# The backward half of a fused S4 and SwiGLU kernel on one Trainium2 core: which engine and which queue does which piece of it

## The chip, the cores and the metric

The kernel runs on one core of one Trainium2 chip. A core has a matrix engine (TensorE, PE in the profile; its weight loads are PEld), VectorE (DVE), ScalarE (ACT), GpSimd (POOL) and a queue engine SyncE (SP). Each runs its own list of instructions in order, and they wait for each other through semaphores. SP, ACT and POOL can issue DMAs, which 16 DMA engines carry out. The metric is the device time of one execution in microseconds (us).

## The reference

Forward and backward of one block on x = A_u of 2048 rows (L) by 576 columns (D):

```python
xn = layernorm(x)
s  = causal_conv(xn, K) + xn * Dskip      # K[d, l] = Re sum_n C exp(dt A l) dt B
h  = silu(xn @ w1) * (xn @ w3)            # 2048 x 4608
g  = silu(h @ w2)
out = x + s * g
```

The state has N = 128 complex entries for each column, and the convolution is causal over all 2048 rows. The outputs are `out` and the gradients of all inputs for a given grad_out: x (out_1), A, B and C, real and imaginary (out_2 to out_7), log dt (out_8), Dskip (out_9), w1, w3 and w2 (out_10 to out_12). Inputs and outputs are bf16, sums are float32.

## The kernel before, in words

The forward comes first: the prologue with layernorm, tables and spectra; the FFN's hidden layer (L719 to L722) beside the generation of the convolution kernel; and the forward tail with the convolution in four quarters of 144 columns, the w2 product (L784) and the transposes of the gradient of the FFN's output into `goT` (L820). The forward leaves in DRAM: the gate and up products (`GI_dram`), h (`H_dram`), spectra of the input and the kernel (`UH_dram`, `KH_dram`), `GS_dram` (the gradient of s), and for the parameters `Q_dram` and `PZ_dram`.

`backward` (L1067) has three strands.

- **The FFN groups.** 4608 hidden columns in 18 groups of FG = 256. `phase6_load` (L1125) brings w2 rows by POOL's queue (`w2r`, L1139) and transposes them on SP (`w2T`, L1123), loads gate and up (`gg_n`, `h_n`) by POOL's queue, and works out silu and its derivative on ACT (L1149, L1151), the gate's factor and h on DVE (L1153, L1154). `phase6_group` (L1157) forms ph = goT x w2T on PE (L1172), empties it on ACT (L1175, `gh`), multiplies on DVE (L1178), stores the two gradients `GU_dram` and `GG_dram`, and makes the weight gradients: w2 (L1200, emptied at L1204) and w1, w3 (L1218, L1227; emptied on ACT at L1221, stored by POOL at L1222).
- **The convolution and the parameters**, woven between the groups. `conv_bwd_quarter` (L866) does a quarter of the columns: it loads spectra (`a3`, variants by DVE at L590 to L592), transforms the gradient (L564, ACT L568), multiplies spectra on DVE (`cmul_acc`, L601 to L610), and transforms back on PE (L582), twice. The first result is the kernel's gradient: 16 tiles of 144 columns a quarter, each written by four strided ACT activations (L926, L927) into `gk_st`, which is stored. The second gives the gradient of xn, added by DVE to `gx` (L947) and stored in `GXN_dram`. `param_quarter` (L950) takes chunks of 16 columns, 36 in all: `qT` is transposed from `Q_dram` on SP, `pz` is loaded by ACT's queue, PE multiplies (L970), DVE multiplies by pz into a tile of 1024 (L977) and reduces it (L979) into `S_all`. After the last chunk `phase5_final` (L984) loads the six rate matrices (L81) and works out for five blocks of columns the gradients of A, B, C and log dt (L996 to L1054).
- **The input stage**, `phase6_inputs` (L1234), after the groups: 16 tiles of 128 rows. The two gradients are transposed from DRAM (`ggc`, `guc`), w1 and w3 are transposed too (12 of 36 chunks early in a pool of their own, `wA`; 24 at the stage's start, `wTB_w`), 144 matmuls sum into `px` (L1262), DVE adds `gxs` (L1265), and `ln_bwd_tile` (L1269 to L1291) finishes the row tile.

What runs first is set by a scheduler at build time: `self.at(us)` sets a priority for what is issued after it, and the order on each engine follows priorities and dependences. `backward(560, 36, 90, 15, 18, ...)` gives these for the groups (36 apart), the convolution's quarters (90), the parameter chunks (15) and the input tiles (18). Tile pools with a number of buffers set when a buffer is free again. `self.dma` alternates SP and ACT.

Of the kernel before, what the change touches and what calls it, by code (L numbers as in the profile page):

```python
# [16 lines left out]
P = 128  # L17
# [43 lines left out]
class K:  # L61
# [246 lines left out]
    def compute_W(self, pool, c, dsz):  # L308
        nc, cfg = self.nc, self.cfg
        N = cfg.N  # L310
        v = slice(0, dsz)
        Wr = pool.tile([P, N], FP32, name="Wr_c")
        Wi = pool.tile([P, N], FP32, name="Wi_c")
        t2 = pool.tile([P, N], FP32, name="Wt2")
        dtc = self.dt_col[v, c:c + 1]
        nc.vector.tensor_tensor(out=Wr[v], in0=self.C_re[v, c, :], in1=self.B_re[v, c, :], op=ALU.mult)
        nc.vector.tensor_tensor(out=t2[v], in0=self.C_im[v, c, :], in1=self.B_im[v, c, :], op=ALU.mult)
        nc.vector.tensor_tensor(out=Wr[v], in0=Wr[v], in1=t2[v], op=ALU.subtract)
        nc.vector.tensor_scalar(out=Wr[v], in0=Wr[v], scalar1=dtc, scalar2=None, op0=ALU.mult)
        nc.vector.tensor_tensor(out=Wi[v], in0=self.C_re[v, c, :], in1=self.B_im[v, c, :], op=ALU.mult)  # L320
        nc.vector.tensor_tensor(out=t2[v], in0=self.C_im[v, c, :], in1=self.B_re[v, c, :], op=ALU.mult)
        nc.vector.tensor_tensor(out=Wi[v], in0=Wi[v], in1=t2[v], op=ALU.add)
        nc.vector.tensor_scalar(out=Wi[v], in0=Wi[v], scalar1=dtc, scalar2=None, op0=ALU.mult)
        return Wr, Wi

# [262 lines left out]
    def spectrum_variants(self, A2, Az):  # L588
        nc = self.nc
        nc.vector.tensor_copy(out=A2[:, :, 1], in_=A2[:, :, 0])  # L590
        nc.vector.tensor_copy(out=A2[0:1, :, 1, 0, :], in_=Az[0:1, :, 0, :])
        nc.vector.memset(Az[0:1, :, 0, :], 0.0)  # L592

# [245 lines left out]
    def ssm_bwd_conv(self, T0, TQ, ps):  # L839
# [3 lines left out]
        with self.tc.tile_pool(name="b_k", bufs=1, side="right") as kp, self.tc.tile_pool(name="b_z", bufs=2, side="right") as zp:  # L843
            self.at(T0)
            self.lcol = kp.tile([P, LT], FP32, name="lcol")
            nc.vector.tensor_scalar(out=self.lcol[:], in0=self.irow[:, 0:LT], scalar1=float(P),
                                    scalar2=self.pcol[:, 0:1], op0=ALU.mult, op1=ALU.add)
            nc.vector.tensor_scalar(out=self.lcol[:], in0=self.lcol[:], scalar1=1.0 / 512, scalar2=None, op0=ALU.mult)
            self.ones_col = kp.tile([P, 1], BF16, name="ones_col")
            nc.vector.memset(self.ones_col[:], 1.0)  # L850
            for g in range(4):
                self.conv_bwd_quarter(g, kp, zp, ps, T0 + g * TQ, TQ)

    def ssm_bwd_params(self, T0, TC, S_all, ps):
        cfg = self.cfg
        D, LT = cfg.D, cfg.LT
        with self.tc.tile_pool(name="g_k", bufs=1, side="right") as gkp, self.tc.tile_pool(name="g_q", bufs=2, side="right") as qp:
# [5 lines left out]
            for g in range(4):  # L863
                self.param_quarter(g, gz, S_all, qp, ps, T0 + TC * g * D // 64, TC)

    def conv_bwd_quarter(self, g, kp, zp, ps, T0, TQ):  # L866
# [10 lines left out]
        for b in range(NB):  # L877
            a3 = kp.tile([P, 3, KT, W], BF16, name=f"a3_{b}")
            nc.sync.dma_start(out=a3[:, 1], in_=self.UH_dram[g, b, :, 0])
            nc.sync.dma_start(out=a3[:, 0], in_=self.UH_dram[g, b, :, 1])  # L880
            A2[b], Az[b] = a3[:, None, 1:3], a3[:, None, 0]
            self.spectrum_variants(A2[b], Az[b])
# [6 lines left out]
        for b in range(NB):  # L889
            prod = zp.tile([P, KT, W], BF16, name="gsxn")  # L890
            for tt in range(KT):
                t = b * KT + tt
                nc.vector.tensor_tensor(out=prod[:, tt, :].rearrange("p (h d) -> p h d", h=2),
# [12 lines left out]
        for i in range(NB - 1, -1, -1):  # L906
            self.at(T0 + TQ * (0.2 + 0.1 * (NB - 1 - i)))
# [12 lines left out]
            for oc in range(KT):  # L920
                t = i * KT + oc
                pt = ps.tile([P, 512], FP32, name="et_ps")
                self.idft_tile(pt, ZZ, oc)
                for h in range(2):
                    pv = pt[:, h * W // 2:(h + 1) * W // 2].rearrange("p (c d) -> p c d", d=8)
                    nc.scalar.activation(out=st[:, :, 0, :, h, t], in_=pv, func=ACT.Copy, scale=1.0 / 512)  # L926
                    nc.scalar.activation(out=st[:, :, 1, :, h, t], in_=pv, func=ACT.Copy, scale=self.lcol[:, t:t + 1])  # L927
# [7 lines left out]
        for j in range(NB):  # L935
            self.at(T0 + TQ * (0.6 + 0.1 * j))
# [3 lines left out]
            gx = zp.tile([P, KT, W], FP32, name="gx")  # L940
            nc.vector.tensor_tensor(out=gx[:], in0=gs[:, j * KT:(j + 1) * KT, :],
                                    in1=self.dskip_row[:, None, cs].to_broadcast([P, KT, W]), op=ALU.mult)
            for oc in range(KT):
                t = j * KT + oc
                pt = ps.tile([P, 512], FP32, name="et_ps")
                self.idft_tile(pt, Z, oc)
                nc.vector.tensor_tensor(out=gx[:, oc, :], in0=pt[:, 0:W], in1=gx[:, oc, :], op=ALU.add)  # L947
            nc.scalar.dma_start(out=self.GXN_dram[:, j * KT:(j + 1) * KT, cs], in_=gx[:])

    def param_quarter(self, g, gz, S_all, qp, ps, T0, TC):  # L950
# [3 lines left out]
        for cc in range(NQ):  # L954
# [6 lines left out]
            qT = qp.tile([P, 16, N], BF16, name="qT")  # L961
            self.nat_transpose(qT[:], self.Q_dram[ch])
            pz = qp.tile([P, 3, 16, AV], BF16, name="pz")
            nc.scalar.dma_start(out=pz[:], in_=self.PZ_dram[:, ch])
            for h in range(2):
# [8 lines left out]
                for s in range(2):  # L974
                    pr = qp.tile([P, 2, 8, 2, AV], FP32, name="pr_q")
                    for r in range(2):
                        nc.vector.tensor_tensor(out=pr[:, r], in0=T[r][:], in1=pz[:, s + r, h * 8:h * 8 + 8, :][:, :, None, :]  # L977
                                                .to_broadcast([P, 8, 2, AV]), op=ALU.mult)
                    nc.vector.tensor_reduce(out=S_all[:, 2 * s:2 * s + 2, d0:d0 + 8].rearrange("p k d -> p d k"),  # L979
                                            in_=pr[:].rearrange("p r d k a -> p d k r a"), op=ALU.add, axis=AX.XY)  # L980

    def phase5_final(self, out, big, S_all, ps2):
        nc, cfg = self.nc, self.cfg
        D, DT, N = cfg.D, cfg.DT, cfg.N  # L984
        aps = self.aps
        fp = out.enter_context(self.tc.tile_pool(name="gf", bufs=2, side="right"))
        fo = out.enter_context(self.tc.tile_pool(name="gfo", bufs=3, side="right"))
        pp = out.enter_context(self.tc.tile_pool(name="gfp", bufs=1, side="right"))
        if True:
            self.load_rates(pp)  # L990
            glogdt = big.tile([P, DT], FP32, name="glogdt")
            nc.vector.memset(glogdt[:], 0.0)
            for c, (do, dsz) in enumerate(cfg.dch):
                pt = ps2.tile([P, 4, N], FP32, name="et_ps")
                for kd in range(4):
                    nc.tensor.transpose(pt[0:dsz, kd, :], S_all[:, kd, do:do + dsz], self.ident_f[:])  # L996
                ST = fp.tile([P, 4, N], FP32, name="ST")
                nc.scalar.copy(out=ST[0:dsz], in_=pt[0:dsz])
                v = slice(0, dsz)
                S1r, S2r, S1i, S2i = ST[v, 0, :], ST[v, 1, :], ST[v, 2, :], ST[v, 3, :]  # L1000
                Wr_t, Wi_t = self.compute_W(fp, c, dsz)
                Wr, Wi = Wr_t[v], Wi_t[v]
                dtc = self.dt_col[v, c:c + 1]
                grho = fp.tile([P, N], FP32, name="grho")
                gth = fp.tile([P, N], FP32, name="gth")
                t1 = fp.tile([P, N], FP32, name="ft1")
                nc.vector.tensor_tensor(out=grho[v], in0=Wr, in1=S2r, op=ALU.mult)
                nc.vector.tensor_tensor(out=t1[v], in0=Wi, in1=S2i, op=ALU.mult)
                nc.vector.tensor_tensor(out=grho[v], in0=grho[v], in1=t1[v], op=ALU.subtract)
                nc.vector.tensor_tensor(out=gth[v], in0=Wr, in1=S2i, op=ALU.mult)  # L1010
                nc.vector.tensor_tensor(out=t1[v], in0=Wi, in1=S2r, op=ALU.mult)
                nc.vector.tensor_tensor(out=gth[v], in0=gth[v], in1=t1[v], op=ALU.add)
                nc.vector.tensor_scalar(out=gth[v], in0=gth[v], scalar1=-1.0, scalar2=None, op0=ALU.mult)
                for src, oname in ((grho, "out_2"), (gth, "out_3")):
                    ob = fo.tile([P, N], BF16, name="gout")
                    nc.vector.tensor_scalar(out=ob[v], in0=src[v], scalar1=dtc, scalar2=None, op0=ALU.mult)
                    self.dma(aps[oname][do:do + dsz, :], ob[v])
                acc1 = fp.tile([P, 1], FP32, name="acc1")
                acc2 = fp.tile([P, 1], FP32, name="acc2")
                junk = fp.tile([P, N], FP32, name="junk")  # L1020
                nc.vector.tensor_tensor_reduce(out=junk[v], in0=grho[v], in1=self.A_re[v, c, :], scale=1.0, scalar=0.0,
# [366 lines left out]
```

## Time and profile before

| | us |
|---|---|
| median of 2 runs | 2061.51 (2052.20 to 2070.82) |
| the profiled execution | 2058.91 |
| its span | 2057.1 |
| FFN groups, first to last weight-gradient store | 794 to 1642 |
| convolution backward | about 800 to 1320 |
| parameter chunks | 1319 to 1990 |
| input stage, px matmuls | 1656 to 2017.4 |
| POOL w2r L1139 waiting for w2T transposes | 122.1 |
| ACT gw L1221 waiting for out_dram<-gw | 40.0 |

All times are from one execution. A busy time is the sum of the durations of an engine's instructions; a wait is idle time of an engine put down to what released it. A group of instructions is named by its line, engine, operation and tiles. The mean granted clock of TensorE was 0.947 of full speed.

### The profile page before, as it was taken

How to read it: one execution, taken by the hardware profiler on the slowest of the kernel's cores; microseconds unless marked ns; L12 is line 12 of the kernel's file. 1: busy time of each engine (PE TensorE's matmuls, PEld its weight loads, DVE VectorE, ACT ScalarE, POOL GpSimd, SP SyncE). 2: the span in 40 equal slices, each digit the busy share in tenths (PEclk: the TensorE clock that was granted, in tenths of full speed). 3: DMA queues.
4: the chain of work that ended last, by engine and by line, in shares of the span. 5: the costliest groups of instructions: out<-in, count | busy, mean ns of one | idle time of the engine just before them, and what ended most of it. 6: DMA issues, size and time to landing. Idle time of an engine off the chain costs nothing. (4 is left out here: it accounts for less than half of the span.)

```text
span 2057.1 us, 42197 instructions
## 1 busy us (share of the span) xinstructions
PE 1772.9 (86%) x17174; PEld 1300.8 (63%) x17174; DVE 1428.3 (69%) x2772; ACT 992.8 (48%) x1668; POOL 366.5 (18%) x540
## 2 busy tenths in 40 slices
PE   2889999999699995999898998898899939989992
PEld 1534444444488874778777777786678727767771
DVE  7548888888287723686874868676789635858667
ACT  2778888888445544765646556343355200000000
POOL 4003333333312102111111211222111200000000
PEclk9999999999799997999999999999899969999996
DMA  3678888896957568465563655798898599999970
GB/s 83 204 290 301 306 298 302 290 320 248 283 140 175 136 139 260 125 179 168 165 179 96 195 155 164 196 264 205 183 208 203 163 232 216 198 216 226 208 150 22
DMA packets 595505, 416.06 MB, mean 202 GB/s; under 512 B 404912, under 2 KB 537136, under 8 KB 590704
## 3 DMA queue, kind: packets, MB, share of 16 engines
q1 hardware_dynamic: 539632, 264.00, 53.6%
q0 software_dynamic: 30544, 120.94, 17.2%
q10 hardware_dynamic: 25136, 28.44, 5.5%
q8 instruction: 134, 2.20, 0.4%
q14 instruction: 59, 0.48, 0.1%
HBM read 133.01 MB, written 188.01 MB: 156 GB/s over the span
## 5 line engine op out<-in xcount | busy, mean ns | idle before, releaser
L719 PE MATMUL pgu<-wmB_w,xnT 128*128 128x512 bf16 x1152 | 284.1, 382 | 1.1 <-ACT E_k L392 1.1
L1262 PE MATMUL px<-wTB_w,guc 128*128 128x288 bf16 x1152 | 243.7, 292 | 36.4 <-DMA guc<-GU_dram 24.1
L1262 PE MATMUL px<-wTB_w,ggc 128*128 128x288 bf16 x1152 | 245.3, 292 | 15.0 <-DMA wTB_w<-in_B_w_dram 9.1
L1218 PEld LDWEIGHTS <-xn_bf 128*128 128x128 bf16 x2304 | 226.2, 98 | 48.7 <-issue 20.7
L977 DVE TENSOR_TENSOR pr_q<-et_ps,pz 128x512 f32<-128x512 f32 x288 | 186.6, 680 | 96.2 <-PE et_ps L970 96.0
L1172 PE MATMUL ph<-w2T,goT 128*128 128x256 bf16 x1440 | 192.3, 286 | 8.8 <-ACT gh L1175 6.5
L719 PEld LDWEIGHTS <-xnT 128*128 128x128 bf16 x1152 | 103.5, 98 | 125.2 <-issue 20.9
L1279 ACT ACTIVATE t<-gx 128x576 f32<-128x576 f32 x16 | 10.9, 683 | 346.0 <-DVE gx L1265 311.3
L979 DVE TENSOR_REDUCE S_all<-pr_q 128x16 f32<-128x1024 f32 x144 | 173.9, 1211 | 0.4
L1200 PE MATMUL pgw<-go_o,h_n 128*128 128x288 bf16 x1152 | 160.9, 294 | 8.7 <-DVE h_n L1154 8.7
L1172 PEld LDWEIGHTS <-goT 128*128 128x128 bf16 x1440 | 144.1, 103 | 33.8 <-issue 7.8
L1262 PEld LDWEIGHTS <-guc 128*128 128x128 bf16 x1152 | 114.1, 100 | 68.9 <-DMA guc<-GU_dram 26.1
L1221 ACT CAST gw<-pgw 128x256 bf16<-128x256 f32 x144 | 53.7, 378 | 212.5 <-PE pgw L1218 169.7
L784 PE MATMUL po<-w2g,hc 128*128 128x288 bf16 x1152 | 148.9, 286 | 2.6 <-DMA hc<-H_dram 2.6
L1218 PE MATMUL pgw<-gg_n,xn_bf 128*128 128x256 bf16 x1152 | 132.5, 276 | 14.2 <-ACT gw L1221 14.2
L1262 PEld LDWEIGHTS <-ggc 128*128 128x128 bf16 x1152 | 113.8, 100 | 45.4 <-issue 9.6
L1200 PEld LDWEIGHTS <-h_n 128*128 128x128 bf16 x1152 | 113.9, 100 | 39.0 <-DVE h_n L1154 9.2
L1218 PE MATMUL pgw<-gu_n,xn_bf 128*128 128x256 bf16 x1152 | 132.3, 272 | 3.4 <-ACT gw L1221 2.0
L784 PEld LDWEIGHTS <-hc 128*128 128x128 bf16 x1152 | 111.5, 98 | 30.2 <-DMA hc<-H_dram 3.1
L722 ACT ACTIVATE s_t<-pgu 128x512 bf16<-128x512 f32 x144 | 87.4, 609 | 55.2 <-PE pgu L721 54.7
L1222 POOL DMA_DIRECT2D out_dram<-gw x144 | 77.7, 541 | 187.1 <-ACT gw L1221 184.0
L1175 ACT CAST gh<-ph 128x512 bf16<-128x512 f32 x144 | 83.7, 613 | 50.8 <-PE ph L1172 35.9
(305 smaller groups left out, 3726.1 us busy)
## 6 DMA issues: line engine op xcount, KB each, us to landing
GI_dram<-gu_t POOLq DMA_DIRECT2D x72, 512.0 KB, 5.7
H_dram<-h_t SPq DMA_DIRECT2D x72, 256.0 KB, 5.2
Q_dram<-q_k SPq DMA_DIRECT2D x36, 512.0 KB, 5.3
gg_n<-GI_dram POOLq DMA_DIRECT2D x18, 1024.0 KB, 5.7
h_n<-GI_dram POOLq DMA_DIRECT2D x18, 1024.0 KB, 8.7
GU_dram<-gu_n SPq DMA_DIRECT2D x36, 512.0 KB, 4.2
GG_dram<-gg_n SPq DMA_DIRECT2D x36, 512.0 KB, 7.5
E_dram<-E_k SPq DMA_DIRECT2D x18, 768.0 KB, 3.6
```

The lines of the kernel that those rows point to most:

```text
L719: nc.tensor.matmul(pgu[:, j], lhsT=xnT[:, c, ts], rhs=wm[w][:, c, :], start=(c == 0), stop=False)
L722: nc.scalar.activation(out=s_t[:, :, q, :], in_=pgu[:, 0].rearrange("p (g f) -> p g f", g=ng), func=ACT.Silu)
L784: nc.tensor.matmul(pos[k][:, pi_, 0:pw], lhsT=hcs[k][:, fi, :], rhs=w2[fi][:, po:po + pw], start=(fi == 0), stop=(fi == FT - 1))
L977: nc.vector.tensor_tensor(out=pr[:, r], in0=T[r][:], in1=pz[:, s + r, h * 8:h * 8 + 8, :][:, :, None, :] .to_broadcast([P, 8, 2, AV]), op= ...
L979: nc.vector.tensor_reduce(out=S_all[:, 2 * s:2 * s + 2, d0:d0 + 8].rearrange("p k d -> p d k"), in_=pr[:].rearrange("p r d k a -> p d k r ...
L1172: nc.tensor.matmul(ph[j][:, k, :].rearrange("p (a f) -> p a f", f=P), lhsT=lw, rhs=rh, start=(n == 0), stop=(n == nfull))
L1175: nc.scalar.copy(out=gh[:, j], in_=ph[j][:])
L1200: nc.tensor.matmul(pgw[pi_][:, 0:pw], lhsT=hn[:, tt, fl * P:(fl + 1) * P], rhs=go_o[:, tt, po:po + pw], start=(tt == 0), stop=(tt == LT - 1))
L1218: nc.tensor.matmul(pw_[:, 0:FG], lhsT=self.xn_bf[:, tt, c * P:(c + 1) * P], rhs=nat[:, tt, :], start=(tt == 0), stop=(tt == LT - 1))
L1221: nc.scalar.copy(out=gw[:], in_=pw_[:, 0:FG])
L1222: nc.gpsimd.dma_start(out=aps[oname][c * P:(c + 1) * P, fb:fb + FG], in_=gw[:])
L1262: nc.tensor.matmul(px[pi_][:, 0:pw], lhsT=act[:, fi, :], rhs=wT[part][ai][:, f, po:po + pw], start=(fi == 0 and ai == 0), stop=(fi == FT - ...
```

## The change

In `backward` and what it calls:

- w2: no row loads, no `w2r`; two fixed `w2T` buffers, transposed from DRAM on SP: 512 columns of a row block by one transpose, the other 64 by a second call (it is built as an ordinary copy whose source steps 576 elements).
- h: the DVE product of silu and up (L1154) goes; after the gate's factor is made, `h_n` is loaded again, now from `H_dram`, by POOL's queue.
- Queues: gate and up loads, and all stores of weight gradients, from POOL to ACT; the four full column blocks of a w1 or w3 gradient are collected and stored at once; `pz` from ACT to SP; `GXN_dram` stores from ACT to SP, in two halves.
- Convolution: a third load in place of two DVE copies, with one row fixed by POOL; products `gsxn` and `gx` on POOL; transforms back in pairs of tiles in one PSUM bank; the kernel's gradient written densely by ACT (`gk_sd`) and put into `gk_st` order by POOL; new priorities.
- Parameters: POOL adds the two halves of `pr_q`, DVE reduces 512 elements; three `qT` buffers; `final_block` runs for a block of columns as soon as its chunks are done, with its rates loaded by POOL's queue, in place of `phase5_final` at the end.
- Input stage: 9 chunks of w1 and w3 early, 27 at its start; DVE adds in place into `gxs`, without a permutation.
- `backward(560, 40, 96, 15, 18, ...)`.

The core of the diff (`spectrum_variants` held the three DVE instructions of L590 to L592; in `final_block` the arithmetic is that of `phase5_final` and is left out):

```diff
@@ conv_bwd_quarter
-            nc.sync.dma_start(out=a3[:, 1], in_=self.UH_dram[g, b, :, 0])
-            nc.sync.dma_start(out=a3[:, 0], in_=self.UH_dram[g, b, :, 1])
+            for j, r in ((0, 1), (1, 0), (2, 0)):
+                nc.sync.dma_start(out=a3[:, j], in_=self.UH_dram[g, b, :, r])
-            self.spectrum_variants(A2[b], Az[b])
+            nc.gpsimd.tensor_copy(out=a3[0:1, 2, 0, :], in_=a3[0:1, 0, 0, :])
+            nc.gpsimd.memset(a3[0:1, 0, 0, :], 0.0)
...
-                nc.vector.tensor_tensor(out=prod[:, tt, :].rearrange("p (h d) -> p h d", h=2),
+                nc.gpsimd.tensor_tensor(out=prod[:, tt, :].rearrange("p (h d) -> p h d", h=2),
...
-            for oc in range(KT):
-                t = i * KT + oc
+            sd = sp.tile([P, KT, 2, W], BF16, name="gk_sd")
+            for o2 in range(0, KT, 2):
+                t = i * KT + o2
                 pt = ps.tile([P, 512], FP32, name="et_ps")
-                self.idft_tile(pt, ZZ, oc)
+                for j in range(2):
+                    self.idft_tile(pt[:, j * W:(j + 1) * W], ZZ, o2 + j)
+                nc.scalar.activation(out=sd[:, o2:o2 + 2, 0, :], in_=pt[:, 0:2 * W].rearrange("p (t d) -> p t d", t=2),
+                                     func=ACT.Copy, scale=1.0 / 512)
+                for j in range(2):
+                    nc.scalar.activation(out=sd[:, o2 + j, 1, :], in_=pt[:, j * W:(j + 1) * W], func=ACT.Copy,
+                                         scale=self.lcol[:, t + j:t + j + 1])
+            for k in range(2):
                 for h in range(2):
-                    pv = pt[:, h * W // 2:(h + 1) * W // 2].rearrange("p (c d) -> p c d", d=8)
-                    nc.scalar.activation(out=st[:, :, 0, :, h, t], in_=pv, func=ACT.Copy, scale=1.0 / 512)
-                    nc.scalar.activation(out=st[:, :, 1, :, h, t], in_=pv, func=ACT.Copy, scale=self.lcol[:, t:t + 1])
+                    nc.gpsimd.tensor_copy(out=st[:, :, k, :, h, i * KT:(i + 1) * KT],
+                                          in_=sd[:, :, k, h * W // 2:(h + 1) * W // 2].rearrange(
+                                              "p t (c d) -> p c d t", d=8))
...
-            nc.vector.tensor_tensor(out=gx[:], in0=gs[:, j * KT:(j + 1) * KT, :],
+            nc.gpsimd.tensor_tensor(out=gx[:], in0=gs[:, j * KT:(j + 1) * KT, :],
...
-                nc.vector.tensor_tensor(out=gx[:, oc, :], in0=pt[:, 0:W], in1=gx[:, oc, :], op=ALU.add)
-            nc.scalar.dma_start(out=self.GXN_dram[:, j * KT:(j + 1) * KT, cs], in_=gx[:])
+                nc.vector.tensor_tensor(out=gx[:, o2:o2 + 2, :], in0=pt[:, 0:2 * W].rearrange("p (t d) -> p t d", t=2),
+                                        in1=gx[:, o2:o2 + 2, :], op=ALU.add)
+            for h in range(2):
+                nc.sync.dma_start(out=self.GXN_dram[:, j * KT:(j + 1) * KT, :].rearrange(
+                    "p t (h g d) -> p t h g d", h=2, g=4)[:, :, h, g], in_=gx[:, :, h * W // 2:(h + 1) * W // 2])
@@ param_quarter
-            qT = qp.tile([P, 16, N], BF16, name="qT")
+            qT = tqp.tile([P, 16, N], BF16, name="qT")
-            nc.scalar.dma_start(out=pz[:], in_=self.PZ_dram[:, ch])
+            nc.sync.dma_start(out=pz[:], in_=self.PZ_dram[:, ch])
...
+                    nc.gpsimd.tensor_tensor(out=pr[:, 0], in0=pr[:, 0], in1=pr[:, 1], op=ALU.add)
                     nc.vector.tensor_reduce(out=S_all[:, 2 * s:2 * s + 2, d0:d0 + 8].rearrange("p k d -> p d k"),
-                                            in_=pr[:].rearrange("p r d k a -> p d k r a"), op=ALU.add, axis=AX.XY)
+                                            in_=pr[:, 0], op=ALU.add, axis=AX.X)
+            self.at(T0 + TC * (cc + 2))
+            ready(ch)
@@ final_block
+        for i, n in enumerate(("A_A_re", "A_A_im", "A_B_re", "A_B_im", "A_C_re", "A_C_im")):
+            nc.gpsimd.dma_start(out=X[v, i, :], in_=aps[n][do:do + dsz, :])
@@ backward
-        FA = 12
+        FA = 9
+            self.w2T = [wp.tile([P, self.FG // P, cfg.DT, P], BF16, name=f"w2T{i}") for i in range(2)]
@@ phase6_load
-            nc.gpsimd.dma_start(out=w2r[:, 0:D], in_=aps["B_w2"][fi * P:(fi + 1) * P, :])
-            self.nat_transpose(w2T[:, fl], w2r[:])
+            self.nat_transpose(w2T[:, fl, 0:nfull], aps["B_w2"][fs, 0:nfull * P])
+            self.nat_transpose(w2T[0:rem, fl, nfull], aps["B_w2"][fs, nfull * P:D])
-        nc.gpsimd.dma_start(out=gg[:], in_=self.GI_dram[gi, :, 0])
-        nc.gpsimd.dma_start(out=hn[:], in_=self.GI_dram[gi, :, 1])
+        nc.scalar.dma_start(out=gg[:], in_=self.GI_dram[gi, :, 0])
+        nc.scalar.dma_start(out=hn[:], in_=self.GI_dram[gi, :, 1])
...
-            nc.vector.tensor_tensor(out=hn[:, sl, :], in0=gu[:, sl, :], in1=hn[:, sl, :], op=ALU.mult)
+        nc.gpsimd.dma_start(out=hn[:], in_=self.H_dram[:, :, gi * FG:(gi + 1) * FG].rearrange("t p f -> p t f"))
@@ phase6_grad13
+            gw = gwp.tile([P, nfull, FG], BF16, name="gw13")
...
-                nc.scalar.copy(out=gw[:], in_=pw_[:, 0:FG])
-                nc.gpsimd.dma_start(out=aps[oname][c * P:(c + 1) * P, fb:fb + FG], in_=gw[:])
+                nc.scalar.copy(out=gw[:, c, :], in_=pw_[:, 0:FG])
+            nc.scalar.dma_start(out=aps[oname][0:nfull * P, fb:fb + FG].rearrange("(c p) f -> p c f", p=P), in_=gw[:])
```

## The prediction

> **What bounds the kernel now.** I read the page first (busy shares, slices, costliest groups), then a table of windows by stage, then what TensorE (PE) waited for in each stage, then the chain of work that ended last. The page:
>
> ```profile
> PE 1772.9 (86%) x17174; PEld 1300.8 (63%) x17174; DVE 1428.3 (69%) x2772; ACT 992.8 (48%) x1668; POOL 366.5 (18%) x540
> ```
>
> PE is the bound; VectorE (DVE) at 69% isn't, so its removed work is worth only what PE waits for it. By stage (columns: PE, PE load, DVE, ACT, POOL busy with counts, granted clock, DMA share, GB/s):
>
> ```profile
> 800.00:1320.00 520.00, 462.54 (x4663) 394.89 (x4662) 370.07 (x770) 315.59 (x714) 92.40 (x167) 0.96 0.56 167
> 1320.00:1645.00 325.00, 289.85 (x3004) 243.59 (x3001) 240.81 (x336) 139.97 (x234) 64.61 (x118) 0.96 0.89 206
> 1645.00:1720.00 75.00, 34.26 (x271) 24.68 (x272) 31.57 (x45) 0.78 (x2) 0.00 (x0) 0.70 1.14 229
> 1720.00:2017.00 297.00, 281.57 (x2604) 223.52 (x2602) 205.41 (x399) 13.06 (x32) 0.00 (x0) 0.98 1.07 194
> 2017.00:2057.00 40.00, 0.72 (x6) 0.33 (x4) 27.16 (x145) 1.50 (x5) 0.00 (x0) 0.56 0.09 20
> ```
>
> The rows are the FFN groups with the conv backward; the groups with the parameters; the start of the input stage; its steady part; the tail. PE idles 57.5, 35.2, 40.7, 15.4 and 39.3 us in them: 188 us is all that any edit here can win. What PE waited for between 700 and 1645:
>
> ```profile
> PE et_ps L582 <- ACT gk_st L927: 20.7, 22, 3.2
> PE pgw L1218 <- ACT gw L1221: 16.2, 8, 5.0
> PE et_ps L970 <- DMA qT<-Q_dram: 14.7, 4, 8.9
> PE ptr L820 <- DVE goT L824: 12.1, 4, 9.4
> PE et_ps L582 <- DVE gx L947: 9.8, 4, 3.6
> PE pgw L1200 <- DVE h_n L1154: 8.7, 1, 8.7
> PE ph L1172 <- ACT gh L1175: 6.5, 5, 2.6
> ```
>
> Columns: us in total, times, longest. The first, fifth and sixth are aimed at directly. The tail, from the chain:
>
> ```profile
> 1991.64 0.41 SPq L81
> 1992.10 3.76 DMA A_im_bf<-in_A_A_im_dram
> 1995.87 2.52 DMA C_re_bf<-in_A_C_re_dram
> ...
> 2037.20 0.20 DVE gr L1043
> ...
> 2042.15 0.59 DVE t L1286
> 2042.76 0.77 DVE t L1289
> 2043.55 0.82 DVE o L1291
> ```
>
> After the last parameter reduction the six rate matrices are loaded, then DVE does all five blocks of phase5_final from 1998 to about 2040, in front of the last layernorm tile. The last px matmul ends at 2017.4, so 39.7 us are tail.
>
> **What the Trainium skill says.** "DMA: Bandwidth & Descriptors", Rules for kernel authors: an access pattern whose last dim isn't contiguous becomes one descriptor per element. Same page, Issuing engines are not separate DMA queues: moving a DMA to another engine's queue saves only issue time; the 16 engines stay shared. Same page, Bandwidth (Measured): about 10.5 ns per packet, a price used below. "SBUF — State Buffer", Who interferes with whom: a DVE instruction with two SBUF inputs and a GpSimd (POOL) instruction that reads SBUF block each other. The trace of before agrees with the second in that the input stage's DMA share stays near 1.1 whatever queue issues; it shows none of the others clearly.
>
> **The change, part by part.**
>
> (1) Tail. Each of the five final blocks is issued as soon as its last chunk is reduced, and in PE's program order the parameters now end 4.85 tiles (4.85 x 20.8 us, from 15 px tiles in 311 us) before the end. The last block's loads (3.8+2.5 us) and its fifth of the 42 us of DVE work lie under px matmuls. Left behind the last px: L1265 twice 0.45, L1282 0.75, L1285 0.14, L1286 0.57, L1289 0.75, L1291 0.81 = 3.9, the store about 5.2 (median landing of out_dram<-o), about 1 to close: 10. **39.7 - 10 = -30.** If the parameters end late, the cover is gone and up to 8 us (one block) come back.
>
> (2) Kernel gradients (64 idft tiles). Before: 128 activations at 0.815 and 128 at 0.791 = 162 us of ACT, strided. After: per pair one dense 128x288 (L676 is 0.40) and two 128x144 (L568 is 0.32): 32 x 1.04 = 33 us; POOL does the strided step in 64 copies, off PE's path because only the gK store, then the parameters, want it. Their cost isn't in the trace: between 0.5 us (POOL's smallest copies) and 1.9 us (POOL's 128x640 adds reach 1950 ns), 32 to 122 us of a POOL busy 92 of 520. The 20.7 us of waits go, but PE then meets DVE's product chain: I take **-15**. The halved gx adds (32 at 0.45 for 64 at 0.30): of 9.8 **-6**.
>
> (3) h. 72 DVE products at 0.68 (48 us) become 18 POOL-issued loads of 1 MB, and the single 8.7 us wait of pgw on h_n: **-6**. The load lands in 5.7 to 8.7 us (GI rows) and is wanted half a group (23 us) later. Behind it in POOL's order stand gsxn, gk copies and later the pr adds; it waits for DVE's gg product, a few us.
>
> (4) Weight gradients. 144 + 36 + 36 stores leave POOL (144 x 0.541 = 78 us of issue) for ACT as 36 + 36 + 36, and so do the 36 GI loads. ACT waited 40.0 us for out_dram<-gw with gw's buffers; with three times larger tiles and fewer stores, PE's 16.2 falls by **-10**. New: 144 issues at about 0.55 us (ACTq 619 ns at L81) = 79 us on the engine that empties PSUM, each of which may wait for an earlier transfer. ACT drops 129 in (2), and its busy share in these stages is 61 and 43%: average room is there, moments aren't: **+8**.
>
> (5) Other DVE relief in the conv: gsxn (10.1), gx products (11.8), the copies at L590-592 (8.7) go to POOL or to 16 more UH loads. Nothing directly, as PE rarely waits there; two-input DVE products (L601-610, some 220 us) and POOL's reads of SBUF now block each other; up to half of POOL's new 60 to 150 us could return: **+4**, since DVE is busy only 370 of 520.
>
> (6) Parameters. 144 reductions of 1024 at 1.21 become 512, about 0.65: DVE -80 us; 144 POOL adds of 128x512 f32, near 1.53 (its 128x640 f32 add): 220 us over the 671 us from 1319 to 1990, 6.1 per chunk of 18.6, so POOL isn't the pace. PE waits for pr_q only 0.9 and 3.6: **-3**. The third qT buffer against 14.7: **-5**. Moving pz to SP adds 36 issues to a queue that carries transposes of 3.4 to 5.7 us each: **+3**.
>
> (7) Input stage. wB grows from 24 to 27 chunks of 36: the ten transposes at the start took SP 33.8 us, 12.5% more is **+4**. The contiguous add at L1265: nothing, since DVE waits 114 us for px there.
>
> (8) w2. The row loads and SBUF transposes (1.2 us of SP each) become a DRAM transpose of 512 columns and, for the other 64, a copy whose source steps 576 elements: 128 x 64 = 8192 two-byte elements, 512 per engine if spread over 16, 36 such copies. The w2T buffers are filled a group ahead (47 us), so only traffic counts. Price: 10.5 ns gives 5.4 us each; the mean packet of queue q1 (53.6% of 16 x 2057.1 over 539632 packets) is 33 ns, 17 us each. The one like it before, the load of log_dt (32 two-byte elements per engine), landed in 2.3 us where the quickest 16 KB load took 2.0, so 9 ns; counted against a 1.5 us store it is 25. I take 10.5, and keep 5 to 17 us. Room: the stages of transposes hold a share of 1.14, so the parameter groups have 1.14 x 325 - 0.89 x 325 = 81 us of engine time. In them fall 14 copies, 7 reloads of h (2048 packets of 512 B, 33 ns, over 16: 4.2 us each, 30) less 14 row loads and transposes (about 2 us each, 28). So 14 copies fit up to (81 - 2)/14 = 5.6 us each, and above that each us costs 14/1.14 = 12.3 us. At 5.4 they just fit: **+3**.
>
> Sum: -30 -15 -6 -6 -10 +8 +4 -3 -5 +3 +4 +3 = -53; 2058.9 - 53 = 2006. The conv stage has 57.5 us idle and DVE lighter by about 60 of 370, so some of the small unnamed waits go too: -6. 2000 on the profiled run's scale; the median shown, 2061.5, is 2.6 above it, within the spread of its two runs, and is taken as the same.
>
> **Rivals.** *Small packets become the bound (slower).* At 17 us the parameter groups overshoot by (14 x 17 + 2 - 81)/1.14 = 139 us, the conv groups (22 copies, 593 - 291 us of room) by about 65: 2058.9 + 204 - 53 = 2210. It eats the gain from 5.6 + 56/12.3 = 10.2 us a copy (20 ns an element) and costs 2% from 13.7 us (27 ns). For it: the share is 1.14 already at 1320-1390 and through the input stage. Against: the log_dt load. *Only the tail (same):* PE in the groups stands at 0.89 busy and ACT's new queue returns what gk_st gave: 2058.9 - 30 + 4 = 2033; the six small sources of idle make it possible. *Everything bites:* of 92.7 us of idle in the groups 75 go with the tail: 2059 - 105 = 1954; against it, gh and goT (18.6) aren't touched, and a wait removed on PE uncovers the next producer in the same chain. *The edit on DVE does nothing* is the second case: DVE is never PE's long wait.
>
> **Numbers.** Likeliest case (1965 to 2020) 0.43; everything bites 0.12; only the tail or partly slowed copies (2020 to 2103) 0.22; packets bound 0.23. A measurement of this kernel can tell about 2% from no change, 2020 to 2103. Faster 0.55, same 0.22, slower 0.23. The likeliest's own range is 1965 to 2020; for 8 in 10, 1948 to 2125.
>
> **What would show it.** Right: the tail after the last px near 10 us; no wait on gk_st; L979 near 0.65 us; DVE about 200 us lower; w2T copies landing within 8 us and the share in the parameter groups near 1.1. Wrong: w2T copies landing in 15 us or more, with PE waiting for w2T, qT or guc; PE waiting for ACT while ACT waits for a DMA; pr adds well above 2 us.

## The result and the profile after

The changed kernel takes 2411.95 us (median of 2 runs, 2410.19 to 2413.72) against 2061.51: a ratio of 1.17, 95% interval 1.147 to 1.193. It was forecast at 2000, with 1948 to 2125 as the range; the forecast had the wrong sign. Ratios leave out single runs over 1.5% above the fastest of the same kernel; medians of runs include them. The page after, in the lines that answer to those shown of before:

```profile
PE 1837.2 (76%) x17174; PEld 1330.5 (55%) x17174; DVE 1352.9 (56%) x2538; ACT 939.3 (39%) x1508; POOL 624.3 (26%) x653
...
q1 hardware_dynamic: 849152, 283.42, 70.2%
```

VectorE (DVE) was unloaded less than its share, 69 to 56%, suggests: its busy time fell by 75 us (1428.3 to 1352.9), where the prediction named about 200 as a sign of being right; the rest of the fall is the longer span. It bought nothing: TensorE (PE) fell from 86 to 76%, though its own busy time rose by 64 us while its mean granted clock went from 0.947 to 0.893. Queue q1 carries 309,520 more packets for 19 MB more.

By stage (same columns as before; the groups with the convolution, the groups with the parameters, the start of the input stage, its rest, the tail):

```profile
800.00:1500.00 700.00, 500.13 (x4733) 418.29 (x4733) 353.48 (x574) 272.83 (x568) 187.47 (x192) 0.84 0.99 143
1500.00:1975.00 475.00, 319.84 (x3038) 256.25 (x3038) 228.77 (x388) 134.09 (x228) 123.13 (x106) 0.84 1.07 160
1975.00:2040.00 65.00, 26.88 (x215) 19.07 (x216) 21.96 (x35) 0.00 (x0) 15.19 (x12) 0.66 1.09 218
2040.00:2404.00 364.00, 294.49 (x2594) 229.88 (x2593) 192.70 (x459) 13.66 (x34) 94.77 (x98) 0.92 0.97 160
2404.00:2412.00 8.00, 0.32 (x3) 0.01 (x1) 3.90 (x8) 0.78 (x2) 0.00 (x0) 0.81 0.07 24
```

The convolution's part went from 520 to 700 us, and its DMA share from 0.56 to 0.99 while its GB/s fell from 167 to 143: more busy, moving less. From the first ph to the last weight gradient the groups grew from 847 to 1176 us. The input stage, first px to last, grew from 361 to 417. The tail is 8 us, from 39.7. What PE waited for between 700 and 1975:

```profile
PE ph L1169 <- ACT gh L1172: 74.9, 13, 24.0
PE pgw L1216 <- ACT gw L1218: 70.5, 10, 14.7
PE ph L1169 <- DMA w2T<-in_B_w_dram: 28.2, 2, 20.0
```

The columns are the total in us, the number of waits and the longest. Only the third names w2T. But waits of up to 24 us for ACT, whose copies last 0.6 us, are not ACT's own: something held ACT. SP's queue engine at one such place (start, duration, what):

```profile
1008.50 0.65 SPq L1121 DMA_DIRECT2D w2T<-in_B_w_dram  x1
1009.20 15.89 SPq L1121 DMA_TRANSPOSE w2T<-in_B_w_dram  x1
1025.18 1.47 SPq L874 DMA_DIRECT2D a<-UH_dram  x3
```

The copy of 8192 two-byte elements is issued in 0.65 us, and the transpose behind it can't be issued for 15.9 us, nor anything behind that. The 36 copies and the 36 transposes of w2T land after 15.8 us in the median (2.6 to 22.3); the transposes of the kernel before took 3.2. What a copy does to the rest is plainest where it met little else. This one is issued at 1310.51; the windows of the core, and then all DMA packets from 1312 to 1319:

```profile
1308.00:1312.00 4.00, 4.00 (x36) 3.32 (x34) 4.00 (x8) 2.82 (x3) 3.37 (x1) 1.00 0.85 200
1312.00:1316.00 4.00, 3.01 (x32) 2.52 (x31) 4.00 (x8) 1.77 (x4) 4.00 (x1) 1.00 1.62 3
1316.00:1320.00 4.00, 2.90 (x30) 2.36 (x28) 4.00 (x8) 0.00 (x0) 3.94 (x3) 1.00 1.84 12
...
DMA packets 7904, 0.02 MB, mean 2 GB/s; under 512 B 7904, under 2 KB 7904, under 8 KB 7904
```

For 7 us 7904 packets move 0.02 MB, which is the copy's 8192 two-byte elements but for 288; nothing else moves, though ACT issues a store at 1313.66 and SP stands at the next transpose for 7.42 us from 1311.23. The copy at 1008.50 shared its time with other transfers, and there SP stood longer.

### The profile page after: what moved, and what is told of

Read it like the earlier page. It is cut to its first block, busy times and chain, and to the rows that moved or that the text cites. A ratio compares the mean times of both kernels' runs of the same rounds, so it can differ in the third digit from the quotient of the medians.

```text
span 2411.9 us, 42058 instructions
## 1 busy us (share of the span) xinstructions
PE 1837.2 (76%) x17174; PEld 1330.5 (55%) x17174; DVE 1352.9 (56%) x2538; ACT 939.3 (39%) x1508; POOL 624.3 (26%) x653
## 3 DMA queue, kind: packets, MB, share of 16 engines
q10 hardware_dynamic: 41312, 62.71, 10.5%
## 4 chain that ended last, share of the span: by engine, by line
PE 17%; DMA 15%; DVE 12%; SPq 7%; issue 4%; POOL 3%; ACT 2%; ACTq 0%; POOLq 0%; DVEq 0%
PE px L1258 5%; PE pgw L1216 5%; SPq L1121 5%; DMA w2T<-in_B_w_dram 4%; DMA out_dram<-gout 3%; DMA pz<-PZ_dram 3%; POOL pr_q L989 2%; DVE pr_q L987 2%; PE pgw L1197 2%; PE ph L1169 2%; DVE cm_t L583 1%; DVE S_all L990 1%; DMA a<-KH_dram 1%; PE et_ps L546 1%; DVE cm_t L580 1%
## 5 line engine op out<-in xcount | busy, mean ns | idle before, releaser
L989 POOL TENSOR_TENSOR pr_q<-pr_q 128x512 f32<-128x512 f32 x144 | 190.2, 1323 | 504.1 <-DVE pr_q L987 414.9
L1216 PEld LDWEIGHTS <-xn_bf 128*128 128x128 bf16 x2304 | 238.3, 104 | 147.0 <-issue 106.2
L1169 PE MATMUL ph<-w2T,goT 128*128 128x256 bf16 x1440 | 208.5, 299 | 104.0 <-ACT gh L1172 74.9
L1258 PE MATMUL px<-wTB_w,guc 128*128 128x288 bf16 x1152 | 248.5, 295 | 24.1 <-DMA wTB_w<-in_B_w_dram 12.3
L1197 PE MATMUL pgw<-go_o,h_n 128*128 128x288 bf16 x1152 | 168.6, 299 | 29.7 <-DMA h_n<-H_dram 15.8
L1216 PE MATMUL pgw<-gu_n,xn_bf 128*128 128x256 bf16 x1152 | 148.5, 291 | 54.5 <-DVE gu_n L1175 23.1
L1216 PE MATMUL pgw<-gg_n,xn_bf 128*128 128x256 bf16 x1152 | 144.1, 288 | 47.4 <-ACT gw L1218 47.4
L1274 ACT ACTIVATE t<-gxs 128x576 f32<-128x576 f32 x16 | 11.0, 684 | 387.4 <-DVE gxs L1261 373.6
L990 DVE TENSOR_REDUCE S_all<-pr_q 128x16 f32<-128x512 f32 x144 | 98.8, 686 | 100.7 <-POOL pr_q L989 100.7
L704 POOL DMA_DIRECT2D GI_dram<-gu_t x72 | 68.7, 954 | 216.4 <-DVE gu_t L700 171.4
```

What stands on the lines that cost most here:

```text
L704: nc.gpsimd.dma_start(out=self.GI_dram[fb * ng:(fb + 1) * ng, :, :, i0:i0 + NT, :].rearrange("g p u t f -> p u g (t f)"), in_=gu_t[:].rear ...
L989: nc.gpsimd.tensor_tensor(out=pr[:, 0], in0=pr[:, 0], in1=pr[:, 1], op=ALU.add)
L1169: nc.tensor.matmul(ph[j][:, k, :].rearrange("p (a f) -> p a f", f=P), lhsT=lw, rhs=rh, start=(n == 0), stop=(n == nfull))
L1197: nc.tensor.matmul(pgw[pi_][:, 0:pw], lhsT=hn[:, tt, fl * P:(fl + 1) * P], rhs=go_o[:, tt, po:po + pw], start=(tt == 0), stop=(tt == LT - 1))
L1216: nc.tensor.matmul(pw_[:, 0:FG], lhsT=self.xn_bf[:, tt, c * P:(c + 1) * P], rhs=nat[:, tt, :], start=(tt == 0), stop=(tt == LT - 1))
L1258: nc.tensor.matmul(px[pi_][:, 0:pw], lhsT=act[:, fi, :], rhs=wT[part][ai][:, f, po:po + pw], start=(fi == 0 and ai == 0), stop=(fi == FT - ...
```

## The experiments

Theory 1: the element copies' own time on the DMA engines. Theory 2: ACT, issuing DMAs now, is blocked. Theory 3: POOL's new work stands in the way. Each group of runs was timed beside its own runs of the kernel before (medians 2037 to 2054 us), so between groups I compare ratios.

**Same bytes, whole runs.**

```diff
-            self.nat_transpose(w2T[0:rem, fl, nfull], aps["B_w2"][fs, nfull * P:D])
+            nc.sync.dma_start(out=w2T[0:rem, fl, nfull], in_=aps["B_w2"][(gi * nfl + fl) * P:(gi * nfl + fl) * P + rem, 0:P])
```

> The changed kernel with the 64-column remainder of w2 copied as 64 contiguous runs of 256 bytes instead of 8192 two-byte elements; same bytes, queue, semaphores and count, but the wrong values of w2 land there, so the w2 remainder of ph is not the reference's. Theory 1 (the elements' time on the 16 DMA engines, about 36 x 16 us, sets the loss): falls by over 300 us, to 1990 to 2080, and w2T copies land in under 5 us. Theory 2 (ACT blocked by issuing DMAs): falls only by what ACT waits for w2T, 88 us, to about 2320. Theory 3 (final blocks and pr adds on POOL hold up the input stage): the input stage stays near 430 us long, total not below 2100.

Measured: 2179.73 us, ratio 1.0627 (1.0558 to 1.0696). q1 in this run:

```profile
q1 hardware_dynamic: 556544, 283.42, 56.1%
```

Against the changed kernel that is 292,608 packets (36 x (8192 - 64), one an element) and 0.702 x 2411.9 - 0.561 x 2179.2 = 471 us of all 16 engines less: an estimate of 25.7 ns a packet, 13 us a copy, in the sum of packet times. The w2T copies and transposes now land after 3.4 us in the median. Of the loss, 0.107 of the ratio goes with the elements, some 220 us, where theory 1 had forecast over 300; some 130 us do not, and the input stage is still 415 us long, so theory 3 has a share.

**w2's rows as before**, in the changed kernel.

```diff
-            self.nat_transpose(w2T[:, fl, 0:nfull], aps["B_w2"][fs, 0:nfull * P])
-            self.nat_transpose(w2T[0:rem, fl, nfull], aps["B_w2"][fs, nfull * P:D])
+            nc.gpsimd.dma_start(out=w2r[:, 0:D], in_=aps["B_w2"][fi * P:(fi + 1) * P, :])
+            self.nat_transpose(w2T[:, fl], w2r[:])
```

> The changed kernel with w2's row loads by POOL and transposes from SBUF as before; all else as changed. Theory 1: within 20 us of the contiguous-copy run, 1990 to 2080. Theory 2: about 2320. Theory 3: above 2100, with the loss in the input stage.

Measured: 2192.02, ratio 1.0689 (1.061 to 1.0768): like the contiguous copy, above theory 1's range.

**The w2 edit alone**, on the kernel before (the diff above, reversed).

> The kernel before with only the w2 edit (transposes from DRAM and the element copies on SP, two fixed buffers). Theory 1: slower than before by 200 to 350 us, 2260 to 2410. Theory 2 (needs ACT's new DMAs): loses under 100 us, below 2160.

Measured: 2303.20, ratio 1.1218 (1.1121 to 1.1315): some 250 us lost without any of ACT's new DMAs. PE waits 79.5 us for gh here too, and 29.5 for w2T.

**ACT's DMAs back on POOL**, copies kept.

```diff
-        nc.scalar.dma_start(out=gg[:], in_=self.GI_dram[gi, :, 0])
+        nc.gpsimd.dma_start(out=gg[:], in_=self.GI_dram[gi, :, 0])
...
-            nc.scalar.dma_start(out=aps["out_12"][fi * P:(fi + 1) * P, :], in_=gw2[:])
+            nc.gpsimd.dma_start(out=aps["out_12"][fi * P:(fi + 1) * P, :], in_=gw2[:])
```

> The changed kernel with gate and up loads and all weight-gradient stores back on POOL's queue, element copies kept. Theory 1: gains under 60 us, above 2350. Theory 2: gains 150 us or more, below 2260.

Measured: 2434.66, ratio 1.187 (1.1789 to 1.195): no gain. Theory 2 falls: with POOL issuing, w2T still lands after 16.2 us in the median.

**The remaining 130 us.** In the contiguous-copy run the input stage shows idle stretches of all engines. Its windows (PE, PE load, DVE, ACT, POOL busy; clock; DMA share; GB/s):

```profile
1952.00:1956.00 4.00, 4.00 (x34) 3.06 (x32) 2.31 (x10) 0.64 (x2) 1.02 (x2) 1.00 2.56 105
1956.00:1960.00 4.00, 0.13 (x2) 0.00 (x0) 0.44 (x1) 0.00 (x0) 1.10 (x3) 1.00 1.85 2
1960.00:1964.00 4.00, 0.00 (x0) 0.00 (x0) 0.00 (x0) 0.00 (x0) 0.00 (x0) 0.68 1.45 2
1964.00:1968.00 4.00, 0.00 (x0) 0.00 (x0) 0.00 (x0) 0.00 (x0) 0.00 (x0) 0.50 1.13 35
```

and what POOL had issued just before, with SP's transpose that then hung:

```profile
1947.63 0.54 POOL L1059 DMA_DIRECT2D out_dram<-gl  x1 [0.17 <-issue]
...
1950.73 0.56 POOL L1039 DMA_DIRECT2D out_dram<-gout  x1 [0.39 <-DVE gout L1036]
1950.74 21.22 SPq L1121 DMA_TRANSPOSE guc<-GU_dram  x1
```

The DMA engines count as busy over 100% and move 2 GB/s. Two suspects: POOL's queue (the stores of `gout`), or the store of `gl`, the block's gradient of log dt, 128 two-byte elements written to DRAM by each of the five final blocks. First I took the first:

```diff
-            nc.gpsimd.dma_start(out=aps[oname][do:do + dsz, :], in_=ob)
+            self.dma(aps[oname][do:do + dsz, :], ob)
...
-                tc.tile_pool(name="gfo", bufs=2, side="right") as fo:
+                tc.tile_pool(name="gfo", bufs=3, side="right") as fo:
```

> The changed kernel with w2's rows as before and the final blocks' gradient stores alternating between SP and ACT with three buffers instead of two, not on POOL. Theory 3a (a store issued by POOL among transposes lands after up to 18 us, and DVE waits for its buffer, 71 us in the contiguous-copy run): input stage shorter by 45 to 70 us, total 2125 to 2150. Rival (the stores only fill time in which PE is held by the serial chain of DVE product, POOL add, DVE reduction): under 15 us, above 2175.

Measured: 2282.32, ratio 1.1162 (1.1116 to 1.1209): some 90 us slower than with rows alone, outside both. On top of it, the reduction back on DVE:

```diff
-                    nc.gpsimd.tensor_tensor(out=pr[:, 0], in0=pr[:, 0], in1=pr[:, 1], op=ALU.add)
-                                            in_=pr[:, 0], op=ALU.add, axis=AX.X)
+                                            in_=pr[:].rearrange("p r d k a -> p d k r a"), op=ALU.add, axis=AX.XY)
```

> The one with rows and final stores as before, and the pr_q halves no longer added on POOL (DVE reduces 1024 elements as before). Theory 3b (the POOL add stands in series: two products 1.2, add 1.3, reduction 0.7 make 3.2 us a step against 2.6): another 30 to 60 us less, about 2080 to 2110; PE's wait for pr_q falls from over 40 us to under 10. Rival (DVE's load matters, and POOL takes 80 us off it): slower by 10 to 40.

then `nc.gpsimd` to `nc.vector` at gsxn, gx and the row fixes:

> The one with the reduction on DVE, and also gsxn, the gx products and the two row fixes of the spectra back on DVE. Theory 3c (POOL's list, in order, delays each quarter's start behind stores and loads[...]): another 15 to 40 us less. Rival (DVE relief in the convolution was worth its price): slower by up to 20.

then h:

```diff
+            nc.vector.tensor_tensor(out=hn[:, sl, :], in0=gu[:, sl, :], in1=hn[:, sl, :], op=ALU.mult)
-        nc.gpsimd.dma_start(out=hn[:], in_=self.H_dram[:, :, gi * FG:(gi + 1) * FG].rearrange("t p f -> p t f"))
```

> The one before, and also h worked out by the DVE product instead of the second load on POOL. Left of the change: dense kernel gradients in pairs, ACT's queue for loads and stores of the groups, final blocks early, third buffers, priorities. Theory 3d (the reload comes late, PE waited 21 us for it): 5 to 25 us less, and the total 2000 to 2050, as the tail's 30 us are won. Rival (new priorities and SP's and ACT's lists hold the groups back): total stays above 2080.

Measured: 2245.61, 2223.47 and 2211.07: each step back gains (37, 22, 12 us), as theories 3b to 3d have it, but on top of a loss that I had not explained; the totals that they forecast, 2080 to 2110 for the first and 2000 to 2050 for the last, are missed. In these runs the groups end at 1684 to 1736 and the input stage is over 500 us long.

Then the second suspect, `gl` gathered and stored once as five contiguous rows:

```diff
-            nc.gpsimd.dma_start(out=aps["out_8"][do:do + dsz].rearrange("(p o) -> p o", o=1), in_=gl[v])
+        nc.tensor.transpose(pt[0:DT, 0:P], glogdt[:], self.ident_f[:])
+        gl = fo.tile([P, P], BF16, name="gl")
+        nc.scalar.copy(out=gl[0:DT], in_=pt[0:DT, 0:P])
+        nc.sync.dma_start(out=self.aps["out_8"][0:nfull * P].rearrange("(c p) -> c p", p=P), in_=gl[0:nfull])
```

(and one more row), in four kernels:

> The changed kernel with w2's rows as before, and the gradient of log dt stored once, after the last final block, as five contiguous rows (transposed by PE) instead of five times as up to 128 two-byte elements. New theory 4 (each of those stores of two-byte elements to DRAM stops the other DMAs for some 15 us, four of them inside the input stage): 40 to 75 us less than with rows alone, 2115 to 2150, and no store of a final block lands later than 10 us. Rival 4b (the slow landings come from POOL's queue standing behind the big transposes): under 15 us of change.

> The version with rows, reductions, conv products and h back on DVE and final stores on SP and ACT, and now the contiguous store of the gradient of log dt. Theory 4: 100 to 160 us less, 2050 to 2110, since there the stopped stores also stood in SP's and ACT's lists ahead of transposes and PSUM emptying. Rival 4b: under 20 us.

> The kernel before with only its last store of the gradient of log dt (512 and 64 two-byte elements, landing 14 us after issue, at 2054.5 of 2057) made as contiguous rows. Theory 4: the end comes 5 to 10 us earlier. Rival 4b (elements to DRAM are not slow by themselves): no change.

> The changed kernel with only the contiguous store of the gradient of log dt; element copies of w2 kept. Theory 4: 40 to 80 us less than the changed kernel, 2330 to 2375. Rival 4b: above 2395.

Measured: 2236.51 (1.0891, 1.085 to 1.0931), 0.020 above rows alone; 2170.39 (1.058, 1.0541 to 1.062), 0.023 less than without the new store, half of the forecast; 2036.50 (0.9908, 0.9877 to 0.9938), 18 us faster than the kernel before, more than the 5 to 10 of theory 4; 2453.33 (1.1946, 1.1915 to 1.1977), not faster than the changed kernel. The gain in the kernel before speaks for theory 4, and `gout` now lands in 1.7 us in the median (maximum 5.4) in the rows version. But two runs don't gain. Windows of the rows version show why:

```profile
1850.00:1875.00 25.00, 14.68 (x157) 11.75 (x158) 15.16 (x25) 0.58 (x1) 10.82 (x9) 0.79 1.02 223
1875.00:1900.00 25.00, 4.21 (x56) 3.13 (x55) 21.69 (x56) 0.00 (x0) 11.32 (x11) 0.50 0.55 126
1900.00:1925.00 25.00, 6.58 (x76) 4.75 (x76) 18.09 (x33) 0.58 (x1) 15.65 (x17) 0.50 0.53 107
1925.00:1950.00 25.00, 4.21 (x56) 3.16 (x56) 22.16 (x62) 0.00 (x0) 11.70 (x11) 0.50 0.24 54
```

PE does 4 to 7 us of work in 25: 288 parameter matmuls in a lump, at DVE's pace, with no px between them. In PE's list of the changed kernel these are spread over px tiles 4 to 11; in this list they all stand after tile 4. Each of the runs that lumped had enlarged the pool of the final blocks (a third buffer, or the 128-column `gl`). My theory 5: that pool no longer fits beside the buffers of the input stage, so tile 4 waits until the parameters are through. I took the same contiguous store through an existing buffer (`name="gout"` instead of `"gl"`); nothing else differs from the run before:

> The changed kernel with w2's rows as before and the gradient of log dt stored once as contiguous rows, through an existing buffer, so that no pool grows and PE's order is that of the rows run (2192). Theory 4 (each store of two-byte elements to DRAM stops other DMAs for about 15 us): 40 to 75 us less, 2115 to 2150. Rival 4b: under 15 us less. If theory 5 (a larger pool made the input stage wait for the parameters, and so the lump) is right, the input stage is no longer 480 us but under 400.

Measured: 2121.52, ratio 1.0397 (1.0329 to 1.0465); PE's list is spread again, the input stage is 379 us. So the pool's size made the lump (that the memory overlaps is inferred), and the five stores of elements cost 0.029, about 60 us. On top of it, with every pool unchanged, the reduction; then gsxn, gx, row fixes and h; then the final stores on SP and ACT:

> The same, and the reduction of 1024 elements back on DVE, no POOL add. Theory 3b (POOL's add stands in series with DVE): 20 to 50 us less than without it, 2070 to 2120, PE's wait for pr_q under 15 us. Rival (DVE's relief is worth its price): slower by 10 to 30.

> The same, and gsxn, gx products, row fixes and h back on DVE too. Left of the change: dense kernel gradients in pairs, ACT's queue in the groups, final blocks early, third qT buffer, priorities. Theory 3c and 3d: another 35 to 60 us less, 2020 to 2070. Rival (what is left holds the groups back): above 2080.

> The same, with the final blocks' stores alternating between SP and ACT, in two buffers. If POOL's queue was the fault of the late stores: 10 to 30 us less. If theory 4 had it all: within 10 us.

Measured: 2102.42 us (ratio 1.0322, 1.0258 to 1.0387), 2065.90 (1.0131, 1.0067 to 1.0194), 2062.60 (1.0112, 1.0055 to 1.017). POOL's add cost 0.008 of the ratio, some 15 us (theory 3b had 20 to 50), POOL's share of the convolution and of h 37, its queue for the stores nothing that can be told. The reason for the first is one step in the contiguous-copy run:

```profile
2004.45 1.88 DVE L987 TENSOR_TENSOR pr_q<-et_ps,pz 128x512 f32<-128x512 f32 x3
...
2005.88 1.27 POOL L989 TENSOR_TENSOR pr_q<-pr_q 128x512 f32<-128x512 f32 x1 [6.77 <-DVE pr_q L987]
2007.18 0.69 DVE L990 TENSOR_REDUCE S_all<-pr_q 128x16 f32<-128x512 f32 x1 [0.85 <-POOL pr_q L989]
```

DVE stands still for 0.85 of POOL's 1.27 us, as the reduction is next in its list: two products, add and reduction last 3.2 us in series where two products and a long reduction took 2.6.

Last, the two terms of the sum that had looked safest, on the groups of the kernel before: the early final blocks, and then the dense gradients (the blocks of the change's diff).

> The groups, the convolution and w2 of the kernel before, with its priorities; of the change only the final blocks issued early (stores on SP and ACT), the third qT buffer, pz on SP, 9 chunks of w1 and w3 early, the contiguous layout of the gradient of xn; the gradient of log dt as contiguous rows. Theory: against the kernel before with contiguous rows alone (ratio 0.991) the tail falls from 29 to about 8 us: ratio 0.978 to 0.986. Rival (the input stage grows by what the tail gives, as it did in the version with all on DVE, 382 against 351 us): ratio 0.989 to 1.00.

> The same with the kernel's gradients written densely by ACT and put in order by POOL, in pairs of tiles. Theory (PE's 20 us of waits for gk_st go): 8 to 20 us less than without. Rival (POOL's strided copies and the pairs' longer turn cost as much): within 5 us or slower.

Measured: 2025.15, ratio 0.9899 (0.9863 to 0.9935), and 2047.56, ratio 0.9999 (0.998 to 1.0017). The rivals had it in both. Early blocks add nothing that can be told to the contiguous store alone (0.9908); by the two intervals a gain of some 10 us can't be ruled out, the forecast ratio of 0.978 to 0.986 can. Dense gradients cost 22 us; ACT's and POOL's rows of that run:

```profile
L932 ACT ACTIVATE gk_sd<-et_ps,lcol 128x144 bf16<-128x144 f32 x64 | 20.7, 379 | 0.0
L929 ACT ACTIVATE gk_sd<-et_ps 128x288 bf16<-128x288 f32 x32 | 13.1, 409 | 37.3 <-PE et_ps L564 37.1
...
L936 POOL COPY gk_st<-gk_sd 128x288 bf16<-128x288 bf16 x64 | 90.0, 1450 | 65.0 <-ACT gk_sd L929 65.0
...
L588 DVE TENSOR_TENSOR Z<-Z,cm_t 128x1152 bf16<-128x1152 bf16 x48 | 40.1, 834 | 0.4
```

ACT's 162 us are 34, and PE's 20 us of waits for gk_st are gone, but PE then waits 20.3 for ZZ and 31.7 for gw (13.4 without). One of DVE's two-input products (L588) went from 0.750 to 0.834 us beside POOL's copies.

Added up in ratios: element copies 0.101, element stores 0.029, POOL's add 0.008, POOL's convolution and h 0.019, dense gradients 0.010 (measured on another base): 0.167. The kernel before has an element store of its own, worth 0.009, so this explains about 0.158 of the 0.170. The rest is inside the interval of the 1.17; the new priorities, the third qT buffer and the paired adds of gx were not tested apart.

## Why the prediction was wrong, point by point

**The step that failed is (8), w2.** It failed twice, in the price and in the room. The price: I took 10.5 ns an element from the Trainium skill's "DMA: Bandwidth & Descriptors", Bandwidth (Measured), which has it from transfers that GpSimd issues, and from one load held against the quickest load. In the sum of packet times it is 25.7 (13 us a copy), the value that the same load gave against a 1.5 us store, which I had put aside. In elapsed time it was less wrong: the copy shown above moved 7904 elements in 7 us, 494 an engine at 14 ns, since packets of one engine overlap.

The room was the larger error. By my own formula, 13 us cost 12.3 x (13 - 5.6) = 91 us in the parameter groups and nothing in the convolution's, where I saw 302 us of engine time free. The runs show 207 us (changed kernel against rows) and 250 (alone on the kernel before). In that last run the groups from the last inverse transform on grew from 324 to 427 us, near the formula, but those with the convolution from 524 to 663. Engine time that is free on average was no room, since while a copy's elements moved, little else did. "Filled a group ahead, so only traffic counts" nearly holds for w2T's own readers (28.2 us of waits) and not for the other transfers: SP's next transpose waits, 15.9 us in the place shown, and loads, stores and buffer releases behind it are late. As an estimate, at the pace of the copy shown 8192 elements take 7.3 us, and 36 such stops would be 261 us, near the 207 to 250, though many of the 36 shared their time.

The slower rival, at 23%, named the right cause. That its 204 us for the copies come near the 207 and 250 is luck: it took 17 us a copy, and laid 139 us in the parameter groups and 65 in the convolution's, where the edit alone shows 103 and 139.

**(1) Tail, -30.** The term was right (39.7 to 8 us) and the gain wasn't. The final blocks moved into the input stage with their stores of `gl`, a DMA that I had not costed: about 60 us. Of the old tail, the same kind of store was 18 us by itself. With both made contiguous, early blocks win nothing that can be told: in the profiled executions the tail goes from 29 to 11 us, the input stage from 351 to 360.

**(2) Dense gradients, -15.** Measured +22. The wait moved to ZZ, and the convolution's two-input products on DVE, whose blocking by POOL (5) priced at +4 in all, took 4 to 11% longer in that run (0.749 to 0.781 for one line, 0.750 to 0.834 for another), which agrees with the Trainium skill's "SBUF — State Buffer", Who interferes with whom. How much of the 22 us that is was not separated. The halved gx adds (-6) were not tested apart; PE's wait for gx was 1.2 us with rows and the contiguous store, 9.8 before.

**(3) and (5), h and the convolution on POOL, -2 together.** Measured +37 together; in the runs with the lump, 22 for the convolution's part and 12 for h. PE waited 20.7 us for the reloaded h in the contiguous-copy run, more than the 8.7 that the edit was to remove, but only 5.0 in the run from which the 37 were measured, beside 11.2 for POOL's gsxn. So these waits are not the whole 37.

**(6) Parameters, -5.** Measured some +15 for the add. I compared POOL's 6.1 us with a chunk of 18.6, its throughput; what counts is that its 1.3 us lie between two instructions of DVE. The third qT buffer (-5) was not tested apart; up to 1975 us PE waited 7.5 us for qT in the contiguous-copy run, 17.0 before.

**(4) ACT's queue, -2.** With loads and stores of the groups back on POOL's queue, and the copies still in, the time stayed (ratio 1.187 against 1.170): within what can be told. The prediction's reading that the share stays near 1.1 "whatever queue issues" was a weak test: from 1720 to 1820 us of the kernel before, SP's queue had 97.7% and ACT's 18.8%. **(7) wB, +4:** PE waited for wTB_w 18 to 26 us in all runs, 21 before; nothing to tell.

The gains that I summed were mostly waits of PE. In the case that was tested apart, gk_st, other producers took the wait over; the prediction had held this against "everything bites", and against its own sum only in part (15 of the 20.7 us).

## What to carry to other kernels

Look first at how a DMA is cut: a copy whose last dim isn't contiguous went element by element here, and while its elements moved, little else did, so "prefetched early" is no cover for the other transfers. Work handed to another engine in the middle of a chain cost its latency, though that engine's share of the span was small. When an experiment changes a pool, compare the order of the engines' lists before the times: here some 512 bytes a partition moved the ratio from 1.0397 to 1.0891, about 100 us.

## What the runs showed of the hardware that I had not expected

- A copy of 8192 two-byte elements from DRAM into SBUF kept all other transfers of the core from moving for 7 us where it was shown alone (7904 packets and 2 GB/s from 1312 to 1319 us, with a store of ACT issued at 1313.66). In the sum of packet times an element took 25.7 ns of an engine. Why the others stand still was not tested.
- A store of 128 two-byte elements to DRAM by POOL's queue landed after 18 to 22 us, one of 64 after 10 to 11. In the kernel before, stores of 512 and of 64 elements by SP, issued 0.4 us apart, both landed after 14 us, and q1 moved 636 packets from 2040 to 2042 us and 52 in the 12 us after that: most of the landing passed with little moving. Beside such a store, from 1956 to 1964 us of the contiguous-copy run, only 60 packets started, and SP's transpose hung. The mechanism behind it was not tested.
- A DMA share above 1 says nothing of work done: 1.14 stood beside 229 GB/s in the kernel before and 1.45 beside 2 GB/s here. It sums the times of packets, which overlap.
